# Turning the q tiles of an attention kernel: TensorE transposes or DMA transposes

## The chip, the cores and the metric

The kernel runs on one core of one Trainium2 chip. The metric is the device time of one execution in microseconds (us). TensorE's matrix unit is called PE here, VectorE DVE, ScalarE ACT, GpSimd POOL, and SP is the SyncE queue that issues most of the DMAs.

## What is computed

The reference is an attention with a threshold, followed by a two-layer perceptron. In numpy, with B = 8 batches, H = 8 heads, S = 576 positions and D = 64:

```
scores = matmul(q, k^T) / sqrt(64)
keep   = scores >= max(scores) - tau            # per row, tau = 0.02
attn   = exp(scores - max) where kept, else 0, divided by its row sum
x      = matmul(attn, v), heads side by side    # 4608 tokens x 512
h      = x @ w_in                               # 512 -> 2048
out    = max(0.01 * h, h) @ w_out               # 2048 -> 512
```

Inputs and output are float32.

## The kernel before, in words

**Steps.** The attention runs in 144 steps, 18 per batch. A step takes 128 query rows of one pair of heads (row block `blk`, pair `p`, half `c`: 16 steps a batch), and two tail steps per batch take the last 64 query rows of two pairs each. The main loop (L482 to L522) runs over n and, in iteration n, writes down in a fixed order: the loads due at n (`loads_at`), the exponentials of step n-1, scores and `copy_min` of step n, the evacuation of an earlier pv, POOL work due at n (`pool_at`) around the threshold of step n, the weights of step n-1, and for every second step the reciprocal, `widen` and `turn_w`; then stores, one unit of layer 1, the turns due at n (`turns_at`), two units of layer 2, and pv (four iterations after the pair's second step). The schedule is manual: each engine executes its instructions in this order, and so does SP with its DMAs.

**Scores.** `scores` (L202) multiplies qT and kT with head dimension on the partitions. To keep float32 accuracy with fp16 operands, q and k are each split into a high and a low fp16 part; three products (high-high, low-high, high-low) are accumulated in PSUM as 64x288 pieces. `copy_min` (L220) has DVE copy the scores to SBUF, scaled and negated, with the row minimum.

**Exponentials and weights.** A step has two heads, h = 0 and 1. In the usual form ACT computes `e` (L254) and DVE applies the threshold and sums (L264). For a "steep" step, head 1 goes another way: ACT does a Prelu with a slope of 1e20 (L250) and then the exponential with the row sum (L251), and DVE does nothing for that head. L479 decides: a step is steep when its number is below 12 or when no turn is due in the next iteration (`turns_at`).

**The weights' transpose.** After every second step `turn_w` (L279) has SP issue one DMA transpose of 20 blocks of 128x128 (10 for a tail step) from w to wT; steps 0 to 7 of the first batch use TensorE instead (`turn_w_pe`). One of the blocks holds the reciprocals, widened by POOL (L273). `pv` (L295) multiplies wT with v, and DVE evacuates it (L326; L316 for tails).

**q and k on their way to qT and kT.** Raw q and k come by DMA (`load_main` L75, `load_tails` L84; v by L93 and L100). A batch has ten units: k and q of each of four pairs, and the two tails. For later batches POOL scales a unit by 64 (`split_scale`, L138), makes the high half (`split_high`, L144) and the low half (`split_low`, L148). The halves lie in a ring of four buffers (`half`). `turn` (L162) then transposes a unit on PE, 16 transposes of 128 columns into PSUM (L177), and ACT copies the result to qT or kT (L188). L391 to L403 set when: unit i of batch b is turned in iteration `base + 4 + 18*i//10` (b = 1: `9 + 3*i//2`), where base is the first iteration of the batch before; POOL's split stands two and three iterations ahead. In the middle batches the turns thus fall in iterations 4, 5, 7, 9, 11, 13, 14, 16, 18 and 20 counted from base, and the q units of the four pairs are those of 5, 11, 14 and 18.

**The perceptron.** When four pairs of a row block are done, its 256 tokens go into a queue: `layer1` (L337) takes 16 matmuls and an ACT Prelu at a time (L347, L349), `layer2` (L354) eight matmuls (L360), and a finished group is copied by ACT (L366) and stored by SP (L375, L378).

**The SP queue.** SP issues all loads after the first ones, all `turn_w` transposes and all stores, in the order of the loop above. A DMA that waits for its data holds everything behind it.

Of the kernel before, what the change touches and what calls it, by code (L numbers as in the profile page):

```python
# [38 lines left out]
def kernel(  # L39
# [10 lines left out]
    nc = tc.nc  # L50
# [3 lines left out]
    MAIN = 512  # L54
# [20 lines left out]
    def load_main(b, s, which, eng=None, parts=1):  # L75
        t = sb.tile([128, 4, 256], FP32, tag="raw", bufs=4, name="raw")
        n = 4 // parts
        for i in range(parts):
            (eng or nc.sync).dma_start(
                out=t[:, ds(n * i, n), :],  # L80
                in_=SRC[which][b, ds(4 * s + n * i, n), 0:MAIN, :].rearrange("h (p t) d -> p h (t d)", t=4))
        raws[b, s, which] = t

    def load_tails(b, which, eng=None):  # L84
        t = sb.tile([128, 2, 2, 64], FP32, tag="rawt", bufs=2, name="rawt")
        src = SRC[which][b, :, MAIN:S, :].rearrange("(u sh) p d -> u p sh d", u=2)
        for u in range(2):
            (eng or nc.sync).dma_start(out=t[ds(64 * u, 64), :, :, :].rearrange("p s h d -> p (s h) d"), in_=src[u])
        tails[b, which] = t
# [27 lines left out]
    turned, halves, scaled = {}, {}, {}  # L117

    def turned_of(b, which):
        if (b, which) not in turned:  # L120
            turned[b, which] = sb.tile([128, 2, NP, WIDE[which]], FP16, tag=f"{which}T", bufs=2, name=f"{which}T")
        return turned[b, which]
# [7 lines left out]
    def split_scale(key):  # L130
        t = sb.tile([128, 4, 2, 64], FP32, tag="scaled", bufs=2, name="scaled")
        if key[1] == "t":
            src = tails[key[0], key[2]][:, :, :, :]
            dst = t[:, 0:2, :, :]
        else:
            src = pair_of(*key)
            dst = t[:, :, :, :].rearrange("p t h d -> p h t d")
        nc.gpsimd.tensor_scalar(out=dst, in0=src, scalar1=64.0, scalar2=1.0, op0=AX.mult, op1=AX.mult)  # L138
        scaled[key] = t

    def split_high(key):
        n = 2 if key[1] == "t" else 4
        halves[key] = new_half()
        nc.gpsimd.tensor_copy(out=halves[key][:, 0, 0:n, :, :], in_=scaled[key][:, 0:n, :, :])  # L144

    def split_low(key):
        n = 2 if key[1] == "t" else 4
        nc.gpsimd.tensor_tensor(out=halves[key][:, 1, 0:n, :, :], in0=scaled.pop(key)[:, 0:n, :, :],  # L148
                                in1=halves[key][:, 0, 0:n, :, :], op=AX.subtract)
# [12 lines left out]
    def turn(key, copy=None):  # L162
        copy = copy or nc.scalar.copy
        b, p, which = key
        dst, half = turned_of(b, which), halves.pop(key)
        n = 2 if p == "t" else 4
        c0 = 0 if which == "q" else 64
        if p == "t":
            c0 = MAIN if which == "q" else 0
            tp = ps.tile([128, 2, 2, 2, 64], FP16, tag="h", bufs=2, name="tp")  # L170
        else:
            tp = ps.tile([128, 2, 4, 128], FP16, tag="h", bufs=2, name="tp")
        for x in range(2):
            for t in range(n):
                for h in range(2):
                    o = tp[ds(64 * h, 64), x, :, t, :] if p == "t" else tp[ds(64 * h, 64), x, t, :]
                    nc.tensor.transpose(o, half[:, x, t, h, :], ident[:, :])  # L177
        if p == "t":
            for x in range(2):
                copy(out=dst[:, x, :, ds(c0, 64)], in_=tp[:, x, :, :, :].rearrange("d u s p -> d (u s) p"))  # L180
            if which == "k" and b:
                nc.gpsimd.tensor_copy(out=dst[:, :, :, 576:640], in_=dst[:, :, :, 0:64])
            elif which == "k":
                for x in range(2):
                    nc.vector.tensor_copy(out=dst[:, x, :, 576:640],
                                          in_=tp[:, x, :, :, :].rearrange("d u s p -> d (u s) p"))
        else:
            copy(out=dst[:, :, p, ds(c0, 512)], in_=tp[:, :, :, :].rearrange("d x t p -> d x (t p)"))  # L188

# [190 lines left out]
    loads_at, turns_at, pool_at = {}, {}, {}  # L382

    def at(d, n, f):
        d.setdefault(n, []).append(f)

    def units(b):
        u = [(b, p, w_) for p in range(NP) for w_ in "kq"]
        return u[:2] + [(b, "t", "k")] + u[2:] + [(b, "t", "q")]

    for b in range(1, B):  # L391
        base = PERB * (b - 1)
        for i, (s, w_) in enumerate(((0, "k"), (0, "q"), (1, "k"), (1, "q"))):
            at(loads_at, base + ((-2, 0, 5, 7)[i] if b > 1 else (3, 4, 8, 9)[i]),
               lambda b=b, s=s, w_=w_: load_main(b, s, w_))
        for i, w_ in enumerate("kq"):
            at(loads_at, base + (2, 12)[i] + 4 * (b == 1), lambda b=b, w_=w_: load_tails(b, w_))
        for i, key in enumerate(units(b)):
            n_ = base + 4 + 18 * i // 10 if b > 1 else 9 + 3 * i // 2
            at(pool_at, n_ - 3, lambda key=key: split_scale(key))  # L400
            at(pool_at, n_ - 3, lambda key=key: split_high(key))
            at(pool_at, n_ - 2, lambda key=key: split_low(key))
            at(turns_at, n_, lambda key=key: turn(key))  # L403
    for b in range(B):
        base = PERB * (b - 1)
        if b:
# [52 lines left out]
    for key in first[:3]:  # L459
        split_now(key)  # L460
    turn(first[0])
    turn(first[1], nc.vector.tensor_copy)
    turn(first[2])
    for key in first[3:5]:
# [91 lines left out]
```

## Time and profile before

| What | Value |
|---|---|
| median of three runs | 521.77 us (521.43, 521.77, 523.34) |
| the profiled execution | 523.44 us |
| its span, first to last instruction | 521.7 us |
| granted TensorE clock, mean | 0.989 |
| packets moved by DMA | 220697, 87.76 MB; 190912 of them under 512 B |
| `turn_w` transposes on SP | 76, median 5.2 us from issue to landing |
| turns on PE (L177) | 1152 transposes, mean 229 ns of one |
| copies of turned q by ACT (L188) | 28, mean 1006 ns |

A row of the profile names line, engine, operation, output and inputs. "Busy" is the union of the time in which an engine executed; matmuls are pipelined, so neighbours overlap and the time that one costs is the distance between starts. DMA share is the mean busy share of the 16 DMA engines; it can go above 1 in a short window because packets overlap. The chain is the work followed back from the last instruction, at each step to what released it. "Landing" is the time at which a DMA's completion semaphore was full.

### The profile page before, as it was taken

What the parts mean: (1) busy time and instruction counts of PE and PEld (TensorE: products, weight loads), DVE (VectorE), ACT (ScalarE), POOL (GpSimd) and SP (SyncE); (2) the same over time, 40 slices, a digit from 0 to 9 for tenths busy, and PEclk for the clock granted to TensorE, in tenths of its full rate; (3) what the DMA queues carried; (4) which work ended last, traced back from release to release, by engine and by line L of the source; (5) the groups of instructions that cost most, each with busy time, mean ns of one, the idle gap of its engine ahead of it and who ended that gap; (6) DMA issues with size and microseconds to landing.
All of it is one profiled execution on the core that took longest, in us unless ns stands there. A gap on an engine that the chain in (4) does not pass through costs nothing.

```text
span 521.7 us, 19307 instructions
## 1 busy us (share of the span) xinstructions
PE 485.7 (93%) x7904; PEld 342.0 (66%) x7904; DVE 422.7 (81%) x1200; ACT 431.9 (83%) x733; POOL 331.5 (64%) x545
## 2 busy tenths in 40 slices
PE   5777887999999999999999999999999999999996
PEld 3454665667767766677666766667666766667773
DVE  4899998999999878988899888988899888888100
ACT  5699896998988978998889888998889889999541
POOL 4956699787777767677667777687667872222000
PEclk9899899999999999999999999999999999999999
DMA  8992975989968998889979988879969975757611
GB/s 244 249 230 48 175 171 112 177 193 203 230 116 172 200 204 177 168 152 231 191 146 182 194 199 188 163 155 233 186 149 184 195 158 135 127 102 151 134 43 62
DMA packets 220697, 87.76 MB, mean 168 GB/s; under 512 B 190912, under 2 KB 217536, under 8 KB 220608
## 3 DMA queue, kind: packets, MB, share of 16 engines
q1 hardware_dynamic: 217648, 82.07, 75.3%
q0 software_dynamic: 2688, 4.19, 4.4%
q8 instruction: 62, 1.02, 0.8%
q14 instruction: 27, 0.22, 0.1%
q10 hardware_dynamic: 272, 0.26, 0.1%
HBM read 36.70 MB, written 9.44 MB: 88 GB/s over the span
## 4 chain that ended last, share of the span: by engine, by line
PE 65%; DVE 16%; DMA 7%; ACT 6%; POOL 3%; issue 2%; DVEq 0%; POOLq 0%
PE hp L347 20%; PE o L360 18%; PE sc L217 17%; DVE s L225 8%; DMA wT<-w 7%; PE pv L304 6%; DVE w L264 5%; PE tp L177 4%; ACT e L254 1%; ACT s L250 1%; DVE x L326 1%; ACT kT L188 1%; DMA raw<-in_k_dram 1%; POOL half L148 1%; ACT osb L366 1%
## 5 line engine op out<-in xcount | busy, mean ns | idle before, releaser
L225 DVE TENSOR_SCALAR_CACHE_REDUCE s<-sc 128x576 f32<-128x576 f32 x288 | 205.2, 750 | 46.0 <-PE sc L217 40.5
L264 DVE SCALAR_TENSOR_TENSOR w<-s,th,e 128x576 f16<-128x576 f32 x210 | 177.2, 866 | 1.9 <-DMA wT<-w 1.7
L254 ACT ACTIVATE e<-s,mn 128x576 f16<-128x576 f32 x210 | 155.7, 774 | 1.5 <-DVE s L225 1.3
L360 PE MATMUL o<-wout,g 128*64 128x512 f16 x1152 | 147.5, 379 | 0.7 <-ACT osb L366 0.7
L217 PE MATMUL sc<-kT,qT 64*128 64x288 f16 (+1 forms) x1920 | 139.8, 290 | 7.8 <-DVE s L225 7.5
L347 PEld LDWEIGHTS <-win 128*64 128x64 f16 x2560 | 118.4, 110 | 33.0 <-issue 30.7
L347 PE MATMUL hp<-x,win 128*64 128x256 f16 x2048 | 136.8, 277 | 0.0
L349 ACT ACTIVATE g<-hp 128x512 f16<-128x512 f32 x144 | 85.1, 591 | 58.8 <-PE hp L347 58.2
L217 PEld LDWEIGHTS <-qT 64*128 64x128 f16 (+1 forms) x1920 | 78.6, 98 | 61.4 <-issue 46.4
L232 POOL TENSOR_SCALAR th<-mn 128x2 f32<-128x2 f32 x130 | 54.9, 422 | 84.4 <-DVE s L225 56.6
L360 PEld LDWEIGHTS <-g 128*64 128x64 f16 x1152 | 62.1, 110 | 31.3 <-issue 1.5
L148 POOL TENSOR_TENSOR half<-scaled,half 128x512 f16<-128x512 f32 (+1 forms) x75 | 81.5, 1087 | 1.7
L144 POOL CAST half<-scaled 128x512 f16<-128x512 f32 (+1 forms) x75 | 62.5, 834 | 4.8 <-POOL th L232 0.2
L273 POOL CAST w<-rec 128x256 f16<-128x256 f32 (+1 forms) x84 | 32.0, 381 | 52.2 <-DVE rec L270 50.0
L304 PE MATMUL pv<-wT,v 128*64 128x256 f16 (+1 forms) x960 | 54.1, 248 | 9.8 <-DMA wT<-w 5.2
L250 ACT ACTIVATE s<-s,th 128x576 f32<-128x576 f32 x78 | 60.3, 773 | 3.4 <-POOL th L232 1.9
L251 ACT ACTIVATE w<-s,minus_tau 128x576 f16<-128x576 f32 x78 | 60.5, 775 | 2.8
L304 PEld LDWEIGHTS <-v 128*64 128x64 f16 x960 | 40.8, 111 | 29.9 <-DMA wT<-w 11.5
L177 PE MATMUL tp<-ident,half 128*64 128x128 f16 x1152 | 49.3, 229 | 7.6 <-ACT half L158 5.2
L138 POOL TENSOR_SCALAR scaled<-raw 128x512 f32<-128x512 f32 x60 | 48.3, 805 | 7.8 <-DMA raw<-in_k_dram 5.9
L177 PEld LDWEIGHTS <-half 128*64 128x64 f16 x1152 | 42.3, 116 | 11.8 <-ACT half L158 5.9
L188 ACT COPY kT<-tp 128x1024 f16<-128x1024 f16 x32 | 32.3, 1008 | 5.6 <-PE tp L177 5.6
(39 smaller groups left out, 278.8 us busy)
## 6 DMA issues: line engine op xcount, KB each, us to landing
vraw<-in_v_dram SPq DMA_DIRECT2D x16, 512.0 KB, 5.1
out_dram<-osb SPq DMA_DIRECT2D x16, 512.0 KB, 3.4
raw<-in_k_dram SPq DMA_DIRECT2D x14, 512.0 KB, 4.7
raw<-in_q_dram SPq DMA_DIRECT2D x14, 512.0 KB, 4.8
win<-in_moe_w_in_dram POOLq DMA_DIRECT2D x4, 512.0 KB, 10.9
wout<-in_moe_w_out_dram POOLq DMA_DIRECT2D x4, 512.0 KB, 9.1
wT<-w SPq DMA_TRANSPOSE x76, 5.2
raw<-in_k_dram SPq DMA_DIRECT2D x4, 256.0 KB, 4.3
```

Source lines behind the costliest of these rows:

```text
L144: nc.gpsimd.tensor_copy(out=halves[key][:, 0, 0:n, :, :], in_=scaled[key][:, 0:n, :, :])
L148: nc.gpsimd.tensor_tensor(out=halves[key][:, 1, 0:n, :, :], in0=scaled.pop(key)[:, 0:n, :, :], in1=halves[key][:, 0, 0:n, :, :], op=AX.sub ...
L177: nc.tensor.transpose(o, half[:, x, t, h, :], ident[:, :])
L217: nc.tensor.matmul(out=o, lhsT=lhs, rhs=turned[st.b, "k"][rows, kx, pair, ds(key0, 288)], start=(i == 0), stop=(i == 2), skip_group_check= ...
L225: nc.vector.tensor_scalar(out=st.s[:, h, :].rearrange("p (a b) -> p a b", a=2), in0=st.sc[h][:, :, 0:288], scalar1=-1.0 / UNIT, scalar2=No ...
L250: nc.scalar.activation(out=z, in_=z, func=AF.Prelu, bias=st.th[:, h : h + 1], scale=-1.0, alpha=1e20)
L254: nc.scalar.activation(out=st.e[:, h, :], in_=st.s[:, h, :], func=AF.Exp, bias=st.mn[:, h : h + 1], scale=-1.0)
L264: nc.vector.scalar_tensor_tensor(out=st.w[h], in0=st.s[:, h, :], scalar=st.th[:, h : h + 1], in1=st.e[:, h, :], op0=AX.is_le, op1=AX.mult, ...
L304: nc.tensor.matmul(out=o, lhsT=v16[st.b % 2][:, st.p + u, blk, :], rhs=rhs, start=(i == 0), stop=(i == 4), skip_group_check=True)
L347: nc.tensor.matmul(out=hp[ds(64 * u2, 64), jj, :], lhsT=w_in16[:, i, ds(128 * j + 64 * u2, 64)], rhs=g.x[:, i, :], start=(i == 0), stop=(i ...
L349: nc.scalar.activation(out=g.g[:, ds(nj * u, nj), :], in_=hp[:, :, :], func=AF.Prelu, bias=0.0, scale=1.0, alpha=0.01)
L360: nc.tensor.matmul(out=g.o[ds(64 * u2, 64), :], lhsT=g.g[:, j, ds(128 * m + 64 * u2, 64)], rhs=w_out16[:, j, :], start=(j == 0), stop=(j = ...
```

## The change

The q units of the four pairs of batches 1 to 7 are no longer turned by PE. A new function `turn_dma` has SP issue two DMA transposes for each, one for the high and one for the low half, straight from `half` into qT: 4 blocks of 128x128 each. k units, the tails of q and all of batch 0 keep `turn`. The DMAs stand at the head of iteration `n_ + 1 - n_ % 2`, that is in iteration n_ if it is odd and otherwise in the next; in the middle batches these are 5, 11, 15 and 19 counted from base, and 11, 15, 19 and 21 for batch 1. As those units no longer stand in `turns_at`, L479 makes the steps before them steep.

```diff
+    def turn_dma(key):
+        b, p, which = key
+        dst, half = turned_of(b, which), halves.pop(key)
+        for x in range(2):
+            nc.sync.dma_start_transpose(
+                out=dst[:, x, p, ds(0 if which == "q" else 64, MAIN)].rearrange("d (t p) -> d t p", t=4),
+                in_=half[:, x, :, :, :].rearrange("p t h d -> p (t h d)"))
...
-            at(turns_at, n_, lambda key=key: turn(key))
+            if key[1] != "t" and key[2] == "q":
+
+                at(loads_at, n_ + 1 - n_ % 2, lambda key=key: turn_dma(key))
+            else:
+                at(turns_at, n_, lambda key=key: turn(key))
```

## The prediction

> **What bounds the kernel now.** I read the page's shares first, then the chain that ended last, then the table of windows cut at the batches (about 59 us each), then the timelines of PE and of the DMA queue (SP) inside one batch. I write w(m) for the wT transpose that iteration m of a batch (m = 0 to 17, 18 for the second tail) issues at L281; pv(m+3) reads it.
>
> ```profile
> PE 485.7 (93%) x7904; PEld 342.0 (66%) x7904; DVE 422.7 (81%) x1200; ACT 431.9 (83%) x733; POOL 331.5 (64%) x545
> ...
> q1 hardware_dynamic: 217648, 82.07, 75.3%
> ...
> PE 65%; DVE 16%; DMA 7%; ACT 6%; POOL 3%; issue 2%; DVEq 0%; POOLq 0%
> ```
>
> PE leads, but DMA holds 7% of the chain. By window (columns: length, busy time of PE, PEld, DVE, ACT, POOL, granted clock, DMA share, GB/s):
>
> ```profile
> 191.50:251.00 59.50, 58.70 (x950) 41.13 (x948) 51.78 (x148) 51.70 (x87) 43.16 (x69) 1.00 0.90 184
> 428.50:486.00 57.50, 57.48 (x858) 39.70 (x854) 45.92 (x136) 52.95 (x98) 13.22 (x35) 1.00 0.69 134
> ```
>
> In a middle batch PE is busy 58.7 of 59.5 us and the 16 DMA engines 0.90. The last batch has no turns and no loads. There w's are issued 5.94 us apart and PE is never idle, so two iterations cost PE 5.94 us; with one turn in them the middle batches show 6.39. A turn therefore costs PE about 0.45 us, not 16 x 229 ns, because transposes overlap. Its neighbours say the same:
>
> ```profile
> 192.57 1.06 PE L347 MATMUL hp<-x,win 128*64 128x256 f16 x16
> ...
> 193.47 0.61 PE L177 MATMUL tp<-ident,half 128*64 128x128 f16 x16
> ...
> 193.91 1.03 PE L360 MATMUL o<-wout,g 128*64 128x512 f16 x8
> ...
> 194.17 1.01 ACT L188 COPY qT<-tp 128x1024 f16<-128x1024 f16 x1
> ```
>
> From the start of tp to the start of o are 0.44 us. PE waits at one place of nearly every batch, pv(17) for w(14):
>
> ```profile
> 241.63 0.40 POOL w L273
> 242.03 0.03 POOL scaled L138
> 242.05 7.84 DMA wT<-w
> 249.89 0.04 issue
> 249.93 0.74 PE pv L304 x10
> ```
>
> A w alone lands in 4.85 us (last batch); here it takes 7.84. Read one by one, the six w(14) of batches 1 to 6 land 0.04 us before their pv starts, and PE stood idle 0, 1.22, 0.44, 0.24, 0.79 and 0.76 us: this transfer has no slack. The cause is the queue ahead of it:
>
> ```profile
> 168.94 3.00 SPq L281 DMA_TRANSPOSE wT<-w  x1
> 171.98 0.58 SPq L375 DMA_DIRECT2D out_dram<-osb  x1
> 172.60 0.44 SPq L93 DMA_DIRECT2D vraw<-in_v_dram  x1
> 173.09 1.64 SPq L88 DMA_DIRECT2D rawt<-in_q_dram  x2
> 175.29 4.95 SPq L281 DMA_TRANSPOSE wT<-w  x1
> 180.28 1.26 SPq L100 DMA_DIRECT2D vrawt<-in_v_dram  x2
> 181.59 1.60 SPq L93 DMA_DIRECT2D vraw<-in_v_dram  x1
> 183.30 4.18 SPq L281 DMA_TRANSPOSE wT<-w  x1
> ```
>
> From w(10) at 168.94 to w(14) at 183.30 SP issues almost without a pause (0.7 us idle), although w(14)'s last input, widen on POOL, was done at 182.37. The engines are full there as well:
>
> ```profile
> 232.00:254.00 22.00, 21.56 (x360) 15.10 (x356) 18.97 (x57) 18.83 (x32) 15.73 (x28) 1.00 0.99 222
> ```
>
> So a batch has two halves: iterations 10 to 17, where the DMA queue ends last, and 18 to 27 (0 to 9 of the next), where PE does.
>
> **The change, part by part.** Durations are from the profiled execution: span 521.67 us, 523.44 with what lies around it, 1.67 above the median 521.77. I work out a difference and put it on the median.
>
> *Removed from PE:* 28 units (q of batches 1 to 7, four pairs) of 16 transposes, 28 x 0.45 = 12.6 us. The four of batch 1 fall at 50 to 90 us, where the chain runs through DVE, POOL and DMA more than PE; I count them at nothing. Batches 2 to 7: 24 x 0.44 = **-10.6 us** if nothing else is late.
>
> *Removed from ACT, moved from DVE:* 28 copies of 1.006 us go. The step before an emptied turn becomes "steep" (L479): 27 steps change one e (774 ns) and one DVE w (866 ns) into Prelu and Exp (773 + 775 ns, and a 187 ns read). Back to back these starts are 0.7 to 0.8 us apart, so a step adds some 0.9 us to ACT and takes 0.9 us from DVE. Per batch ACT stays within 0.5 us of its 51.7 of 59.5, DVE falls by 3.6. The last batch ran every step steep at PE's pace, so ACT hides it. DVE being lighter makes w(14) ready 0.8 us earlier, which is worth nothing while SP gets to it last, and may remove the 0.36 us that PE waits for L316 in five batches: 0 to -1.8, I take **-1**.
>
> *Added to SP and DMA:* 56 transposes of 4 blocks (128x128 each). No row shows one of this size. A 20-block w issues in 3.05 us and lands in 4.85 undisturbed, a 10-block one in 1.34 and 3.35. Above: two DMAs each as dear as the 10-block issue, 2.7 us a unit; below: 0, where the engines are idle. By the difference of the rows, (4.85 - 3.35) / 10 x 8 = 1.2 us of DMA, and 8 x 0.134 to 0.15 = 1.1 to 1.2 us of SP. I take 1.2 for both. It is nearest to these rows.
>
> [...]
>
> *Where each unit's DMAs stand.* They are issued in odd iterations, behind the w of the even one before; what waits behind them on SP is the next loads and the next w.
> 1. q1 (iteration 11) and q2 (turned in 14, now 15) took 0.88 us from PE in the half that ends with w(14). PE only reaches pv(17) sooner and waits: **+5.3 us** (6 x 0.88).
> 2. q1's DMAs go ahead of the v load, w(12) and w(14). SP needs 1.2 us more; its idle time between w(10) and w(14) is 0.5 to 1.9 us (mean 1.1), so w(14) issues 0 to 0.7 later, and full engines deliver it 0 to 1.2 later. I take 0.6: **+3.6**.
> 3. q0's DMAs (iteration 5) go ahead of w(6), whose slack before pv(9) is 0.63, 0.86, 2.00, 1.66, 0.08, 2.41 us. Where 1.2 exceeds it PE waits: 0.57 + 0.34 + 1.12 = **+2.0**.
> 4. q2's stand ahead of w(16) (slack 0.45 to 3.0) and q3's (iteration 19) ahead of w(2), after which the engines fall idle: covered; if not, 0.6 us.
> 5. Scores now wait for DMAs that were issued at least three iterations (9 us) earlier, against a worst landing of 8.2: covered.
> 6. The half buffers (four) are now freed by a landing. In the steady batches POOL asks four or five iterations later. In batch 1, q3's DMAs queue behind the w issued at 89.46 (3.1 us), so leave at 92.6 to 93.8 and land near 95.6; POOL wants the buffer at 93.37 and holds th and widen behind it: 2.2 us. q1's stand before the load and the w at 73.77, which already made PE wait 2.39. Together 0 to +4, I take **+2**.
>
> Sum: -10.6 - 1 + 5.3 + 3.6 + 2.0 + 2 = +1.3 us; 521.8 + 1.3 = **523.0 us**. What a measurement can tell from no change is about 0.5%, 2.6 us.
>
> **The rivals.**
> *PE's gain arrives.* Step 13 being steep lets w(14) leave in time, and the DMAs fit into holes (the engines are idle around 208 to 210, 228 to 230 and 260 to 262). For it: SP issues for some 43 us of the 59 of a batch; the last batch shows PE alone setting the pace. Against it: w(14)'s zero slack six times over. Terms 1 to 3 go: -10.6 - 1 + 2 = -9.6, **512.2 us**.
> *The transfer of w(14) sets a longer batch (slower).* Nothing of q1's DMAs is absorbed: term 2 is 6 x 1.2 = 7.2, the start costs 4, DVE brings nothing: +1.3 + 3.6 + 2 + 1 = +7.9, **529.7 us**. For it: DMA share 0.99 and SP's issues stretched to 4.95 us by full engines. Against: in the batches at 346 and 112 us SP has some 1.9 us idle. It decides from the point where w(14) lands 0.8 us later on average; at 2.7 us a unit another 9 us follow.
> *The change does more or less than it says.* The built program has 448 transposes and 28 copies fewer, 56 DMA transposes more and 105 steep steps for 78, so only the steep steps are hidden in it. Were ACT to bind with them, 0.4 us in each of 27 steps, 11 us, it would look like the second rival; I give it little of that chance.
>
> **How the numbers follow.** Forecast (gain eaten, within 0.5%): 0.38. Slower: 0.35. Faster: 0.27. The range takes in most of both others, 514 to 531.
>
> **What would show it.** PE: 448 fewer tp, busy about 12 us less, idle more. pv(17) still ended by w(14), landing 7.5 to 9 us after issue, PE idle before it 1.5 to 2.5 us a batch. Waits of PE for wT rise from 5 (PEld 11) us to 15 or more in all. POOL shows a wait for a qT transpose near 93 us. DMA share of a middle batch near 1.0. If PE has no wait at pv(17), I am wrong towards fast; if w(2) or w(4) land late too, the backlog lasts the batch and I am wrong towards slow.

## The result, and the profile after

The changed kernel takes 550.72 us (median of four runs, 549.14 to 552.13) against 522.56 us for the kernel before in the same set (four runs, 521.43 to 523.74): a ratio of 1.0538 with a 95% interval of 1.0497 to 1.0579. It is slower by 28 us, where 523.0 us with 514 to 531 were forecast. The profiled execution took 551.08 us, with a span of 549.3. Here and below, slow runs, those more than 1.5% above the fastest of the same kernel, are left out of every time and ratio.

The page of the changed kernel, its lines that answer to those of before (busy time by engine, the main DMA queue, the chain by engine):

```profile
PE 482.1 (88%) x7456; PEld 330.7 (60%) x7456; DVE 403.1 (73%) x1146; ACT 428.7 (78%) x759; POOL 320.4 (58%) x545
...
q1 hardware_dynamic: 248112, 89.42, 84.7%
...
PE 49%; DMA 20%; DVE 12%; ACT 5%; POOL 5%; SPq 4%; issue 3%; POOLq 0%; DVEq 0%; ACTq 0%
```

Every engine does less, and the span is 27.6 us longer. PE's idle time grew from 36.0 us (521.7 - 485.7) to 67.2 (549.3 - 482.1), by 31.2. DMA rose from 7% to 20% of the chain, and SPq, the issuing of DMAs on SP, appears in it with 4%. The waits of PE in the changed kernel (engine, line, what it waited for: us in all, times, longest) say what the idle time is:

```profile
PE pv L312 <- DMA wT<-w: 36.5, 23, 3.3
PE sc L225 <- DVE s L233: 8.0, 16, 1.8
```

Before, the first of these was:

```profile
PE pv L304 <- DMA wT<-w: 5.2, 6, 2.4
```

The wait for wT has grown by 31.3 us, which is all of the added idle time. No new kind of wait of any size appears: scores wait for a q that was turned by DMA once, for 0.8 us. What is late is the old transfer w to wT.

PE's clock changed as well. The granted clock was 0.981 in the profiled run and 0.989 before. Busy time times granted clock, an estimate of PE's work, fell from 480.4 to 472.9 us, by 7.5, while the busy time itself fell by 3.6: about 4 us of PE's gain are missing with the lower clock. It does not order the runs: of the four of the changed kernel the one with the highest clock (0.981) took 551.08 us, one with 0.970 took 549.14. Why the clock is lower no run shows.

Is wT late because it travels longer, or because it leaves later? The DMA issues of the changed kernel (KB each left out by the profile for transposes; the last number is the median time from issue to landing):

```profile
wT<-w SPq DMA_TRANSPOSE x76, 5.7
...
qT<-half SPq DMA_TRANSPOSE x56, 4.0
```

A wT lands 0.5 us later after its issue than before (5.2). That is too little for waits of 1.6 us on average (36.5 / 23). Read one by one over batches 1 to 6, w(12) even lands sooner after its issue, 5.86 us on average against 6.75, but it is issued 9.37 us after w(10), where it was 6.39. So it leaves later. (w(14) lands 7.71 us after its issue, before 7.77; w(16) alone takes clearly longer, 6.79 against 5.52.) SP's timeline in the changed kernel, in the stretch that answers to the one at 168.94 to 183.30 of the kernel before (start, duration, what is issued):

```profile
178.03 3.70 SPq L289 DMA_TRANSPOSE wT<-w  x1
181.76 0.58 SPq L383 DMA_DIRECT2D out_dram<-osb  x1
182.39 2.70 SPq L194 DMA_TRANSPOSE qT<-half  x2
185.14 1.35 SPq L93 DMA_DIRECT2D vraw<-in_v_dram  x1
186.54 1.29 SPq L88 DMA_DIRECT2D rawt<-in_q_dram  x2
187.98 3.84 SPq L289 DMA_TRANSPOSE wT<-w  x1
```

The first row is w(10), the last w(12). SP issues one after the other, with 0.33 us of pauses in all. w(12) starts 9.95 us after w(10); before it was 6.35 (168.94 to 175.29). The two new DMAs (one row, x2) hold SP for 2.70 us, where 1.2 had been put down; a longer w and a longer v load add 0.7 and 0.9, and a shorter tail load and fewer pauses take 0.7 off. PE, in its own timeline, meets w(12) at once:

```profile
193.56 0.74 PE L312 MATMUL pv<-wT,v 128*64 128x256 f16 x10 [1.95 <-DMA wT<-w]
...
201.71 0.74 PE L312 MATMUL pv<-wT,v 128*64 128x256 f16 x10 [1.53 <-DMA wT<-w]
208.77 0.74 PE L312 MATMUL pv<-wT,v 128*64 128x256 f16 x10 [0.93 <-DMA wT<-w]
```

These are the reads of w(12), w(14) and w(16) of one batch. Before, only the second waited. Read one by one over batches 1 to 6, PE waits 10.4 us in all for w(12), 10.7 for w(14), 4.9 for w(16) and 3.7 for w(2) of the next batch. The distance from one w(12) to the next is now 61 to 65 us where a batch took about 59.

Summed over all rows of SP, issuing took 314.9 us before (60% of the span) and 411.9 after (75%): 81.6 of the added 97 are the 56 new DMAs, 1.46 us each (median 1.26, shortest 1.20), and 16.9 are the wT, which issue more slowly (the other rows fell by 1.6). SP did not wait for the split halves: its pauses just before the 56 new DMAs are 2.9 us in all. The windows of the changed kernel over two middle batches (columns as in the prediction):

```profile
190.00:252.70 62.70, 56.61 (x872) 38.47 (x870) 49.17 (x140) 51.20 (x91) 42.12 (x69) 1.00 0.96 184
252.70:316.50 63.80, 59.13 (x949) 40.33 (x950) 49.69 (x142) 51.42 (x92) 41.30 (x71) 0.97 1.02 195
```

The DMA engines' share is 0.96 and 1.02 there, up from 0.90. So two readings are open: the engines carry more (the transfer), or SP cannot issue in time (the issue). The page alone cannot tell which.

### The profile page after: what moved, and what is told of

Read it like the earlier page. It is cut to its first block, busy times and chain, and to the rows that moved or that the text cites. A ratio compares the mean times of both kernels' runs of the same rounds, so it can differ in the third digit from the quotient of the medians.

```text
span 549.3 us, 18484 instructions
## 1 busy us (share of the span) xinstructions
PE 482.1 (88%) x7456; PEld 330.7 (60%) x7456; DVE 403.1 (73%) x1146; ACT 428.7 (78%) x759; POOL 320.4 (58%) x545
## 2 busy tenths in 40 slices
DMA packets 251158, 95.04 MB, mean 173 GB/s; under 512 B 221377, under 2 KB 248001, under 8 KB 251073
## 4 chain that ended last, share of the span: by engine, by line
PE 49%; DMA 20%; DVE 12%; ACT 5%; POOL 5%; SPq 4%; issue 3%; POOLq 0%; DVEq 0%; ACTq 0%
DMA wT<-w 17%; PE hp L355 16%; PE o L368 14%; PE sc L225 13%; DVE s L233 6%; PE pv L312 5%; DVE w L272 3%; SPq L194 3%; DMA rawt<-in_k_dram 2%; PE tp L177 1%; ACT s L258 1%; ACT e L262 1%; POOL v L107 1%; POOL half L148 1%; POOL half L144 1%
## 5 line engine op out<-in xcount | busy, mean ns | idle before, releaser
L272 DVE SCALAR_TENSOR_TENSOR w<-s,th,e 128x576 f16<-128x576 f32 x183 | 156.9, 873 | 8.5 <-DMA wT<-w 6.1
L355 PEld LDWEIGHTS <-win 128*64 128x64 f16 x2560 | 120.7, 112 | 34.6 <-issue 31.4
L355 PE MATMUL hp<-x,win 128*64 128x256 f16 x2048 | 140.7, 282 | 0.0
L262 ACT ACTIVATE e<-s,mn 128x576 f16<-128x576 f32 x183 | 137.1, 770 | 3.2 <-DVE s L233 3.0
L240 POOL TENSOR_SCALAR th<-mn 128x2 f32<-128x2 f32 x130 | 52.3, 403 | 120.2 <-DVE s L233 73.9
L259 ACT ACTIVATE w<-s,minus_tau 128x576 f16<-128x576 f32 x105 | 81.4, 775 | 18.4 <-DMA wT<-w 14.9
L312 PE MATMUL pv<-wT,v 128*64 128x256 f16 (+1 forms) x960 | 55.5, 252 | 39.3 <-DMA wT<-w 36.5
L258 ACT ACTIVATE s<-s,th 128x576 f32<-128x576 f32 x105 | 80.9, 770 | 7.0 <-POOL th L240 5.1
L368 PEld LDWEIGHTS <-g 128*64 128x64 f16 x1152 | 63.6, 111 | 32.3 <-issue 2.7
L138 POOL TENSOR_SCALAR scaled<-raw 128x512 f32<-128x512 f32 x60 | 42.1, 702 | 10.3 <-DMA raw<-in_k_dram 6.1
L177 PE MATMUL tp<-ident,half 128*64 128x128 f16 x704 | 32.1, 234 | 7.5 <-ACT half L158 5.0
L177 PEld LDWEIGHTS <-half 128*64 128x64 f16 x704 | 27.1, 119 | 10.9 <-ACT half L158 5.6
```

The lines of the kernel that those rows point to most:

```text
L258: nc.scalar.activation(out=z, in_=z, func=AF.Prelu, bias=st.th[:, h : h + 1], scale=-1.0, alpha=1e20)
L259: nc.scalar.activation(out=st.w[h], in_=z, func=AF.Exp, bias=minus_tau[:, :], scale=1.0, accum_out=st.sum[h])
L262: nc.scalar.activation(out=st.e[:, h, :], in_=st.s[:, h, :], func=AF.Exp, bias=st.mn[:, h : h + 1], scale=-1.0)
L272: nc.vector.scalar_tensor_tensor(out=st.w[h], in0=st.s[:, h, :], scalar=st.th[:, h : h + 1], in1=st.e[:, h, :], op0=AX.is_le, op1=AX.mult, ...
L312: nc.tensor.matmul(out=o, lhsT=v16[st.b % 2][:, st.p + u, blk, :], rhs=rhs, start=(i == 0), stop=(i == 4), skip_group_check=True)
L355: nc.tensor.matmul(out=hp[ds(64 * u2, 64), jj, :], lhsT=w_in16[:, i, ds(128 * j + 64 * u2, 64)], rhs=g.x[:, i, :], start=(i == 0), stop=(i ...
```

## The experiments

**Theory S (issue):** SP issues in order, each of the new DMA transposes holds it for about 1.25 us however few blocks it has, and every later w leaves that much later. **Theory D (transfer):** the added 128x128 blocks occupy the DMA engines, and every w lands later. **Theory X:** the cost lies in transposing itself, when the engines go back and forth between copying and transposing. **Theory R:** the steep steps and the lighter DVE cost the time. Besides these, the half buffers might have cost something. Each set of runs had the kernel before beside it, whose median lay between 522.56 and 523.82 us, so that times of different sets are set against each other below where differences are large.

**One DMA a unit.** Main columns of qT were laid out so that both halves of a unit merge into one DMA of 8 blocks: the same bytes, half as many DMAs.

```diff
-        for x in range(2):
-            nc.sync.dma_start_transpose(
-                out=dst[:, x, p, ds(0 if which == "q" else 64, MAIN)].rearrange("d (t p) -> d t p", t=4),
-                in_=half[:, x, :, :, :].rearrange("p t h d -> p (t h d)"))
+        nc.sync.dma_start_transpose(
+            out=qmain[b][:, p, :, :].rearrange("d x (t p) -> d (x t) p", t=4),
+            in_=half[:, :, :, :, :].rearrange("p x t h d -> p (x t h d)"))
...
```

> qT of the four pairs is laid out so that both halves of a unit go in one DMA transpose of 8 blocks: 28 DMAs instead of 56, the same 28,672 packets. Theory S (SP's issue time: a DMA transpose occupies SP for about 1.25 us however few blocks it has, and everything behind it in the queue starts later): issue of 8 blocks 1.3 us as for the 10-block tails, 35 us of SP time less, half or more of the 28 us loss comes back: 530 to 538 us. Theory D (the 16 DMA engines' transfer time of the added packets): the same packets, so 547 to 552 us.

Measured: 533.89 us, ratio 1.0201 (1.0147 to 1.0254). 16.8 of the 28 us are gone with the bytes unchanged. (The 28,672 is a count of 128 packets a block; by the profiles the 56 DMAs bring 30,465 packets under 512 B, 221377 less 190912, and the 28, read in the kernel with the tails on ACT, 29,568, 220480 less 190912.) In its trace the 28 issues hold SP for 49.6 us in all (median 1.31, mean 1.77) where the 56 took 81.6, and PE waits for wT little more than half as long as in the changed kernel:

```profile
PE pv L316 <- DMA wT<-w: 19.6, 16, 2.8
```

**One block a DMA.** Still 56 DMAs, at the same places, of one block each.

```diff
-                out=dst[:, x, p, ds(0 if which == "q" else 64, MAIN)].rearrange("d (t p) -> d t p", t=4),
-                in_=half[:, x, :, :, :].rearrange("p t h d -> p (t h d)"))
+                out=dst[:, x, p, ds(0, 128)].rearrange("d (t p) -> d t p", t=1),
+                in_=half[:, x, 0:1, :, :].rearrange("p t h d -> p (t h d)"))
...
```

> As the changed kernel, 56 DMA transposes at the same places, but each turns only one block of 128x128 instead of four; scores of batches 1 to 7 read that block for all row blocks. It leaves out three quarters of the turned q. Theory S: issue stays near 1.2 us, time 545 to 551 us. Theory D: three quarters of the added transfer go, 525 to 532 us.

Measured: 547.68 us, ratio 1.0472 (1.0401 to 1.0543). With a quarter of the bytes nearly the whole loss stays, against theory D. SP's timeline of this kernel, and then that of the one before it, show the issues themselves:

```profile
181.26 2.60 SPq L194 DMA_TRANSPOSE qT<-half  x2
```

```profile
176.77 1.58 SPq L198 DMA_TRANSPOSE qT<-half  x1
...
192.34 1.30 SPq L198 DMA_TRANSPOSE qT<-half  x1
```

Two DMAs of one block each take 2.60 us; one of eight takes 1.30 to 1.58. The medians are 1.23 us for 1 block, 1.26 for 4, 1.31 for 8, and 1.34 for the 10 of a tail's w.

**Nobody turns q.** The units of q in batches 1 to 7 are neither turned by PE nor by DMA; the scores read batch 0's qT.

```diff
-                at(loads_at, n_ + 1 - n_ % 2, lambda key=key: turn_dma(key))
+                at(loads_at, n_ + 1 - n_ % 2, lambda key=key: halves.pop(key))
...
```

> The q units of batches 1 to 7 are turned by nobody: neither PE nor DMA; scores read the turned q of batch 0. It leaves out those turns, and keeps POOL's splits and the steep steps of the changed kernel. If PE's gain is real and the loss is all in the DMAs (S or D): 508 to 514 us. Theory R (the steep steps and the lighter DVE cost the time): 530 us or more.

Measured: 515.28 us, ratio 0.9843 (0.9805 to 0.9882). That is 1.3 us above the expected range, and far from theory R. PE's wait for wT is 6.3 us in its trace. It is what removing the turns brings with no DMA in their place, and the floor from which the DMAs are priced: 550.72 - 515.28 = 35.4 us for 56 DMAs of 4 blocks, 32.4 for 56 of 1 block, 18.6 for 28 of 8 blocks. That is 0.58 to 0.66 us for a DMA, on average, whether it carries 1, 4 or 8 blocks.

**Two tiny DMAs for each transpose.** As the last, q being turned by nobody, but at the place of each transpose of the change stand two plain DMAs of 512 bytes, so that SP issues and the engines have almost nothing to carry.

```diff
-            nc.sync.dma_start_transpose(
-                out=dst[:, x, p, ds(0 if which == "q" else 64, MAIN)].rearrange("d (t p) -> d t p", t=4),
-                in_=half[:, x, :, :, :].rearrange("p t h d -> p (t h d)"))
+            for i in range(2):
+                nc.sync.dma_start(out=tiny[:, 2 * x + i, :], in_=half[:, x, i, 0, 0:2])
...
```

> In place of each of the 56 DMA transposes SP issues two plain DMAs of 512 bytes in all, SBUF to SBUF, at the same place of the queue; q of batches 1 to 7 is turned by nobody and scores read the turned q of batch 0, as in the run without q turns (515.3 us). A plain DMA occupies SP for 0.6 us, so two take the 1.2 us of one transpose, with next to no data and no transposing. Theory S (SP is an in-order queue, its issue time is the cost): 540 to 548 us. Theory X (the cost lies in a transpose itself, in the engines' change between copying and transposing): 515 to 522 us.

Measured: 547.58 us, ratio 1.0462 (1.0414 to 1.0509). The queue's line, the waits and one group of issues of this kernel:

```profile
q1 hardware_dynamic: 233776, 82.13, 73.6%
```

```profile
PE pv L316 <- DMA wT<-w: 31.7, 21, 3.9
```

```profile
184.25 2.69 SPq L198 DMA_DIRECT2D tiny<-half  x4
```

The engines' share of the span is below that of the kernel before (75.3%); times the span it is 401 us, against 393 before and 465 in the changed kernel. The issues take the same 2.69 us a unit, and PE's wait for wT is nearly that of the changed kernel. Theories D and X fall for nearly all of the loss: 32.3 of the 35.4 us above the floor come with next to no transfer and with no transposing. Theory S stands. SP's time is 1.26 us of a landing of 4.0 for one of the new DMAs (medians of the changed kernel), and issues that carry next to nothing made nearly the whole loss.

**The steep steps alone.** The kernel before, with its turns on PE, and the steps of the change steep.

```diff
+            if key[1] != "t" and key[2] == "q":
+                more_steep.add(n_ - 1)
...
-        st.steep = st.n < 12 or not turns_at.get(st.n + 1)
+        st.steep = st.n < 12 or st.n in more_steep or not turns_at.get(st.n + 1)
```

> The kernel before with nothing changed but the rule for steep steps: the 27 steps that the change makes steep are steep, q is turned by PE. Theory R: most of the 28 us, 535 us or more. S and D: ACT has 1.0 us of copy and 0.9 us of steep step in the same iteration, so a little slower at most: 520 to 527 us.

Measured: 520.48 us, ratio 0.9949 (0.9919 to 0.998). They do no harm, which leaves nothing of theory R, and gain about 2.5 us: PE's wait for wT falls from 5.2 us to this, in the waits of this kernel's trace:

```profile
PE pv L304 <- DMA wT<-w: 2.3, 4, 0.9
```

**Five half buffers.** The change with one more `half` buffer (and one `xt` less, to make room).

```diff
-        return sb.tile([128, 2, 4, 2, 64], FP16, tag="half", bufs=4, name="half")
+        return sb.tile([128, 2, 4, 2, 64], FP16, tag="half", bufs=5, name="half")
...
-                xg.x = sb.tile([128, NP, 128], FP16, tag="xt", bufs=2, name="xt")
+                xg.x = sb.tile([128, NP, 128], FP16, tag="xt", bufs=1, name="xt")
```

> The changed kernel with five half buffers instead of four (one buffer of the tail group's x given up for the space). POOL's 5.2 us of waiting for qT DMAs at the start goes. As the prediction's step 6 has it, 2 to 5 us come back: 545 to 549 us; if POOL's wait is hidden behind SP's, 549 to 553 us.

Measured: 546.6 us, ratio 1.0465 (1.0408 to 1.0522), 4.1 us below the change; the two intervals overlap. POOL's timeline of the change had these two waits, and they are gone with the fifth buffer (PE's wait for wT is as it was, 36.6 us):

```profile
87.41 0.61 POOL L144 CAST half<-scaled 128x512 f16<-128x512 f32 x1 [1.43 <-DMA qT<-half]
...
96.00 0.40 POOL L144 CAST half<-scaled 128x256 f16<-128x256 f32 x1 [3.77 <-DMA qT<-half]
```

**Loads moved to POOL (three kernels).** If SP's time is short, taking other DMAs off SP should give the loss back. The 512 KB loads of q, k and v went to GpSimd's queue: in the change, in the kernel with one DMA a unit, and in the kernel before.

```diff
-               lambda b=b, s=s, w_=w_: load_main(b, s, w_))
+               lambda b=b, s=s, w_=w_: load_main(b, s, w_, nc.gpsimd))
...
-                at(loads_at, base + 11 + 3 * s, lambda b=b, s=s: load_v(b, s))
+                at(loads_at, base + 11 + 3 * s, lambda b=b, s=s: load_v(b, s, nc.gpsimd))
```

> The changed kernel with the 512 KB loads of q, k and v of batches 1 to 7 (six a batch) issued by POOL instead of SP; the 56 transposes stay. SP is relieved of about 5 us a batch and POOL gets about 4 us. Theory S: the w transposes start earlier, half of the loss or more comes back, 528 to 540 us. If transfer or the transposes themselves cost the time, nothing changes: 546 to 555 us.

> One DMA transpose of 8 blocks per unit (533.9 us alone) and the loads on POOL. Theory S: the 28 issues of 1.3 us are about what the loads leave free on SP, 516 to 524 us, near or under the kernel before. Otherwise as without the loads' move: 530 to 536 us.

> The kernel before with the same six loads a batch issued by POOL. Theory S: the wait for w(14), 0.2 to 1.2 us a batch, shrinks: 514 to 521 us. If SP's issue time is not what makes w(14) late, or if POOL is hurt by the issues: 522 to 530 us.

Measured: 578.6 us (1.104, 1.097 to 1.111), 571.2 (1.089, 1.0848 to 1.0933) and 556.02 (1.061, 1.0565 to 1.0655). The expectations missed, all three: the move costs 28 to 37 us by itself (against 550.72, 533.89 and the 523.82 of the kernel before), in the kernel before as well, so it says nothing about S. Of the first of the three, the DMA issues:

```profile
wT<-w SPq DMA_TRANSPOSE x76, 6.4
```

A wT lands 6.4 us after its issue, against 5.7 in the change. Why loads from that queue slow the transposes, or POOL's own work, was not settled.

**Tails moved to ACT.** The same idea with another engine and smaller loads: the six 64 KB tail loads of a batch (q, k and v) are issued by ACT.

```diff
-            at(loads_at, base + (2, 12)[i] + 4 * (b == 1), lambda b=b, w_=w_: load_tails(b, w_))
+            at(loads_at, base + (2, 12)[i] + 4 * (b == 1), lambda b=b, w_=w_: load_tails(b, w_, nc.scalar))
...
-            at(loads_at, base + 13, lambda b=b: load_vtails(b))
+            at(loads_at, base + 13, lambda b=b: load_vtails(b, nc.scalar))
```

> The changed kernel with the small loads of batches 1 to 7 (six a batch: tails of q, k and v, 64 KB each, 0.6 us of issue) issued on ACT's queue instead of SP's. All bytes move as before and the 56 transposes stay; SP is relieved of 3.7 us a batch, and ACT gets about as much. Theory S, at the 0.6 us of loss that one issue in SP's queue cost in the runs so far: up to 42 issues x 0.6 = 25 us back, less what ACT loses: 528 to 542 us. If the loss sat in the engines' transfers: 547 to 553 us.

Measured: 537.61 us, ratio 1.0261 (1.0216 to 1.0307). Thirteen us come back from 42 small loads that are carried as before and merely issued elsewhere. PE's wait in this kernel:

```profile
PE pv L312 <- DMA wT<-w: 22.7, 19, 3.1
```

The same move with the turns left on PE and the steep steps of above:

> q turned by PE, the steep steps of the changed kernel (520.5 us), and the small loads on ACT's queue. Theory S: the remaining waits for w(14), some 0.7 us a batch, go: 514 to 519 us. If ACT's 0.5 us per issue bind instead: 521 to 530 us.

Measured: 517.84 us, ratio 0.9898 (0.9869 to 0.9927); against 520.48 without the move. Where w is hardly late (PE waits 2.3 us for it) the move brings 2.6 us, where it is late (36.5) 13. With a fixed price of an issue the two would be equal.

**Which units: pairs 0 and 3, or 1 and 2.** Two hybrids, each with twelve DMAs of 8 blocks in batches 2 to 7 and all other turns on PE. They are the kernel with one DMA a unit with one line changed: pairs 0 and 3 stand in iterations 5 and 19, pairs 1 and 2 in 11 and 15.

```diff
-            if key[1] != "t" and key[2] == "q":
+            if key[1] in (0, 3) and key[2] == "q" and b > 1:
```

> Only q of pairs 0 and 3 of batches 2 to 7 is turned by DMA, one DMA of 8 blocks each, in iterations 5 and 19, where SP has room; pairs 1 and 2, whose DMAs would stand before w(12) and w(16), stay on PE. Theory S: the 12 issues are hidden and PE's 12 x 0.44 = 5.3 us are kept: 514 to 520 us. If every DMA transpose costs its 0.6 us wherever it stands: 523 to 531 us.

```diff
-            if key[1] != "t" and key[2] == "q":
+            if key[1] in (1, 2) and key[2] == "q" and b > 1:
```

> The same number of DMAs as the hybrid of pairs 0 and 3 (batches 2 to 7 only, 12 DMAs of 8 blocks, the rest on PE), but for pairs 1 and 2: in iterations 11 and 15, between w(10) and w(16). A flat price per DMA (each issue costs its 0.6 us of the end wherever it stands) expects what the other hybrid gave, 517 to 522 us. SP's queue with a place (an issue costs where a w without slack follows, nothing where SP has room) expects 12 x 1.3 us, less SP's 0.5 to 1.9 us of room per batch and the 2 to 4 us that PE gains: 526 to 533 us.

Measured: pairs 0 and 3 519.38 us, ratio 0.9923 (0.9898 to 0.9949); pairs 1 and 2 532.99 us, ratio 1.0191 (1.0142 to 1.0241). The waits of PE, in the first hybrid and then in the second:

```profile
PE pv L316 <- DMA wT<-w: 8.7, 10, 2.1
```

```profile
PE pv L316 <- DMA wT<-w: 18.5, 14, 2.5
```

The same twelve DMAs are 13.6 us dearer at one pair of places than at the other, 1.13 us each, most of an issue of 1.31. So the 0.6 us of above is no price of a DMA, but a mean over places. Both numbers are net of the twelve turns that PE is spared (12 x 0.44 = 5.3 us by the prediction's price): pairs 0 and 3 lie 1.1 us below the 520.48 of the steep steps with all turns on PE, in overlapping ranges and with 12 more steep steps instead of 27, and PE's wait for wT is 8.7 us in their trace against 2.3. So even there the DMAs do not look free: they cost a good part of what PE's turns give.

**Together with the tails on ACT.** One DMA for each of the 28 units, and the hybrid of pairs 0 and 3, both with the tails issued by ACT.

> One DMA of 8 blocks per unit for all 28 units, and the tail loads on ACT. SP's theory: 533.9 minus most of the 13 us that the same move gave with two DMAs a unit, bounded by where the queue stops to be late: 521 to 526 us. If something else than SP's time makes the 28 DMAs dear (their data, the half buffers), the move brings less than 5 us: 529 or more.

> The hybrid with pairs 0 and 3 by DMA, and the 64 KB tail loads (q, k and v, six a batch) issued by ACT. The loads take 6 x 0.6 us of SP out of each batch, most of it ahead of w(14). If SP's issue time is what both moves are about, they add: 519.4 - 2 to 3 = 515 to 518 us. If PE alone is left once w(14) has slack, the hybrid's 12 turns fewer show as 5 us below the kernel with PE turns and tails on ACT, 513 us. If the loads on ACT cost ACT as much as they give SP, 519 or more.

Measured: 525.47 us, ratio 1.002 (0.9991 to 1.005), for all 28; 516.56 us, ratio 0.9876 (0.985 to 0.9903), for the hybrid. The second is 1.2% below the kernel before, clear of noise. PE's wait for wT there:

```profile
PE pv L316 <- DMA wT<-w: 5.1, 4, 1.9
```

It can't be told from the 517.84 us of PE's turns with the same move, whose interval overlaps: with PE's wait for wT at 1.0 us there and 5.1 here, the turns moved to DMA are worth little more, 1.3 us. Issuing the q transposes from ACT was not tried.

## Why the prediction was wrong

The sum was +1.3 us; measured is +28. The parts can be set against runs.

*Removed from PE, and term 1: the net about right, its parts not.* -10.6 for the turns and -1 for DVE, with +5.3 of it given back as waits at pv(17), make -6.3. The kernel in which nobody turns q gains 7.7 (522.93 of the kernel before in its set, less 515.28). But in its trace PE's busy time falls by 8.6 us, and its waits for wT grow by 1.1 only (5.2 to 6.3): the +5.3 does not show, and that the net agrees is in part luck. The steep steps are 2.5 us of the gain, where I had allowed 1, and no loss on ACT.

*"Added to SP and DMA": the first step that failed.* I priced a unit by the difference of the 20-block and the 10-block row, per block, "1.1 to 1.2 us of SP", and took it as "nearest to these rows". But the 1.34 us of the 10-block row is not ten blocks of 0.134: from 1 to 10 blocks the issue takes 1.23 to 1.34 us, nearly all of it fixed. A unit is two DMAs, 2.5 us. The upper end I had named, "two DMAs each as dear as the 10-block issue, 2.7 us a unit", was the right one. The kernel with one DMA a unit (median 1.31 us, close to my 1.2, though 1.77 on average) shows what this step was worth: 550.7 - 533.9 = 16.8 of the 27.7 us by which the forecast of 523.0 missed.

*Terms 2 and 4, what stands behind the DMAs: the second.* The other 10.9 us (533.9 - 523.0) stay with one DMA a unit. In that kernel's trace, over batches 1 to 6, PE waits 9.8 us for w(14), where terms 1 and 2 make 12.4 (8.9 on the 3.5 of before): that place is no worse than I had it. What I had at nothing is w(16), 4.7 us, where I called q2's DMAs "covered", and w(12), 2.4 us. q1's DMAs stand ahead of w(12) as well; I had looked only at w(14), which was late before, and never read w(12)'s slack. In the kernel before it is 1.27, 0.97, 1.04, 0.04, 2.36 and 0.50 us. My 1.2 us of SP exceed it by 2.3 us over the six batches, near the 2.4 with one DMA a unit; the 2.70 us that q1's two DMAs hold SP in the row above exceed it by 10.0, near the 10.4 measured in the changed kernel. The sums agree, the single batches less well; read beforehand, this slack would have named the place.

The delay is handed on: w(14), w(16) and in three batches of six w(2) of the next one are late too in the changed kernel, although PE waits for no w(2) where pairs 0 and 3 alone are turned by DMA. That is the case that the prediction named for itself: "if w(2) or w(4) land late too, the backlog lasts the batch". The hybrid of pairs 1 and 2 has just these units: the terms gave them +3.6, with their share of PE's gain cancelled by term 1, and the run shows +9.5 against the kernel before. A further part lies with PE: with one DMA a unit its busy time falls by 5.9 us, not 10.6, at a granted clock of 0.982. That these parts make up the whole of the 10.9 us is not shown.

*Term 3: smaller than priced.* w(6) lands 0.28 to 1.31 us ahead of its pv in batches 1 to 6 of the changed kernel, where all else is late, and PE waits there never. With pairs 0 and 3 alone PE waits 1.4 us for it over the six batches, against my 2.0.

*Term 5: right* but for one wait of 0.8 us.

*Term 6: right in kind, near in size.* POOL waits for a half buffer at 87 and 96 us, 5.2 us in all, the first of them earlier than foreseen; a fifth buffer gives about 4 back against my 2, within overlapping intervals.

*The rivals.* The second named the side and the place: w(14) late and batches longer, "at 2.7 us a unit another 9 us follow". But it spoke of the transfer and of full engines, and the tiny DMAs show 32.3 of the 35.4 us with next to no transfer; and even its sum with those 9 us, 539, stops 12 short, because it counted w(14) alone, and not w(12), w(16) and w(2). The first rival is right only in part: the steep steps by themselves are worth 2.5 us, with less waiting for wT. What was to show in the profile did: 448 fewer tp, pv(17) ended by w(14) at 1.8 us a batch on average. PE's busy time fell by 3.6 us, not 12, at the lower clock.

Not settled: why loads on GpSimd's queue slow this kernel, why the granted clock is lower, and why the wT issue more slowly. Of the last, the new DMAs do not look like the main cause: where nobody turns q the wT hold SP for 245.0 us, 14.2 more than before, against 16.9 more with the change.

## What to carry to other kernels

Price a DMA by two things, its landing and the time it holds the engine that issues it, and take the second from a row of its own size or from the nearest row whole, not per byte: here 1 to 10 blocks held SP for 1.23 to 1.34 us. Then go down the issuing queue from the place where the DMA is put in: read the slack of every transfer behind it up to the first real pause, not only of the one that is late already. In these runs the move of work from a full engine to DMAs lost least at the places where the queue pauses: twelve such DMAs were 13.6 us cheaper there than ahead of transfers with little or no slack, and still no gain over turning on PE could be told. Issuing 42 small loads from another engine did more: it gave 2.6 us with the turns on PE, and 13 with the change.

## What the runs showed of the hardware

- A DMA transpose held SP for 1.23, 1.26, 1.31 and 1.34 us with 1, 4, 8 and 10 blocks of 128x128 (medians), and about 3.05 us with 20 in the last batch of the kernel before, at a DMA share of 0.69: nearly flat up to 10. Single ones took longer, up to 3.5 us with 4 blocks.
- 112 plain DMAs of 512 bytes held SP for 72.6 us in all and cost 32.3 us of time; 56 DMA transposes of one block held it for 76.7 and cost 32.4.
- The 42 loads of 64 KB, moved from SP to ACT, gave 13 us back where PE waited 36.5 us for wT and 2.6 where it waited 2.3.
- 42 loads of 512 KB moved from SP to GpSimd made the kernel before slower by 6.1% (5.65 to 6.55).
